# A routed attention and expert kernel: the third expert's token rows are requested ahead of two weight tiles, and their transposes and copies are written ahead of the weights' steps

## The chip, the cores and the metric

The kernel runs on one core of one Trainium2 chip. Its time is device microseconds of one execution. Each engine of the core works through its own queue of instructions in order: TensorE (PE, with its weight loads listed as PEld), VectorE (DVE), ScalarE (ACT), GpSimd (POOL) and SyncE (SP), which here only issues DMAs. An engine whose next instruction waits holds up all that is queued behind it.

## The reference

Three stages follow one another. An attention over 16 clusters gives 1536 token rows of 512 numbers. A mixture of experts sends each token to one of 8 experts, with two matrix products of 512x1024 and 1024x512. A gated convolution block ends it.

```python
for s in range(S):                       # for each of 2 batches, 768 tokens
    fresh_e = int(np.argmax(logits[b, s]))
    e = fresh_e if s == 0 or local_gate[b, s] < 0.5 else prev_e
    prev_e = e
    p = softmax(logits[b, s])
    h = np.maximum(x[b, s] @ w1[e], 0.0)
    out[b, s] = p[e] * (h @ w2[e])
...
gate = 1 / (1 + np.exp(-causal_conv5(x)))
return gate * (x @ w_val) @ w_out
```

The weights of an expert are 4 tiles of 128x2048 f32: two of w1 and two of w2.

## The kernel before

**Rows by expert.** At the end of attention the token rows (512 numbers, the probability and the token's number, 514 in all) are scattered into `xslots` in DRAM, one region for each expert. `load_x(k)` reads the rows of the expert at place k into a tile `xs`; even and odd places share one buffer each (`xs0`, `xs1`), so the rows of place 2 go into the buffer of place 0. Places 2 to 5 take their expert from a count made on the chip, which SP reads with `value_load`. `do_x(k)` copies the ids and probabilities on DVE, transposes the rows on PE into a single PSUM bank `xp`, and splits the result: `xhi` is the cast by ACT (L1135), `xlo` the remainder by DVE (L1137). Place 2 has 300 rows in pieces of 128, 108 and 64; it does this in two parts, and part 1 needs the bank that part 0 leaves.

**The products.** `do_mm1(k)` runs over two halves q of w1 and two pairs fp of column blocks in each; `do_mm2(k)` follows with w2. The order is mm1(0), mm2(0), mm1(1), mm1(2), mm2(1), mm1(3), mm2(2) and so on. Place 1's first product uses whole f32 tiles (`wone`); place 2's uses tiles that were split into `whi` (ACT, L360) and `wlo` (DVE, L366), and has three terms: xhi by whi, xlo by whi, xhi by wlo.

**The weights' steps.** `w_stage` requests a raw tile `wraw` on SP's queue; when it is in, `w_split` converts it in two halves. These conversions stand in a list `work`; `tick()`, called once for each pair fp and at places of mm2, takes one from it, then two small DVE steps of an overflow table (`late`), then one step of the conversion of the last block's weights (`wspace`: L260 is its load, L230 to L238 its DVE steps). The raw tiles of place 2's w1 are requested at L1251 and at L1275 (`w_stage(stg[0])`); `keep_rows(3)` (L1253) stores a plain copy of the last 384 rows to `xall`. In `do_mm1(0)` the request `load_x(2)` comes after all of these; in `do_mm1(1)` the two parts of `do_x(2)` come after the tick of their pair.

Of the kernel before, what the change touches and what calls it, by code (L numbers as in the profile page):

```python
# [21 lines left out]
E = 8  # L22
# [19 lines left out]
def routed_attention_moe_kernel(  # L42
# [267 lines left out]
    stg = [wstg]  # L310
# [10 lines left out]
    def w_load(j, t):  # L321
        k, i = worder[j]
        if k in AT:
            nc.sync.dma_start(t, wq[4 * AT[k] + i])
        else:
            nc.sync.dma_start(t, wq[bass.ds(turn[k] * 4 + i, 1)].rearrange("o p f -> (o p) f"))
# [5 lines left out]
    def w_stage(at):  # L332
        if pending:
            j = pending.pop(0)
            home[j] = at
            wraw[j] = at.tile([128, 2048], F32, tag="w", name="wraw")
            w_load(j, wraw[j])
# [175 lines left out]
    def keep_rows(gq):  # L513
        nc.sync.dma_start(
            xall[384 * gq:384 * gq + 384, :].rearrange("(t p) c -> p t c", p=128), xnat[:, 3 * gq:3 * gq + 3, :]
        )
# [530 lines left out]
    def tick():  # L1047
        for _ in range(pops[0]):
            if work:
                work.pop(0)()  # L1050
        for _ in range(2 if late else 0):
            if late:
                late.pop(0)()
        if conv and XS.get("ready"):
            conv.pop(0)()
            beats[0] += not late
            if conv and beats[0] % 2:
                conv.pop(0)()
# [15 lines left out]
    def halves(k):  # L1074
        cols = AT[k], E + HALVED.index(AT[k])
        return cols[::-1] if ROWS[AT[k]][0] == PACK else cols

    def load_x(k):
        if k >= E:
            return  # L1080
        n, rows = NT[k], TR[k]
        XS[k] = xs_p.tile([128, -(-WX[k % 2] // 128), XC], F32, tag=f"xs{k % 2}", name="xs")
        if k == 0:
            c = E + HALVED.index(AT[0])
            nc.sync.dma_start(XS[k][:CAPS[0], 0, :], xslots[c * SLOT:c * SLOT + CAPS[0], :])
            return
        if AT.get(k) in HALVED:
            for t, c in enumerate(halves(k)):
                nc.sync.dma_start(XS[k][:TR[k][t], t, :], xslots[c * SLOT:c * SLOT + TR[k][t], :])
            return  # L1090
        if k in AT:
            src = xslots[AT[k] * SLOT:AT[k] * SLOT + CAPS[k], :]
        else:
            src = xslots[bass.ds(turn[k] * SLOT, CAPS[k]), :]
        if FOLD[k] or k == 0:
            for t, r in enumerate(rows):
                nc.sync.dma_start(XS[k][:r, t, :], src[sum(rows[:t]):sum(rows[:t]) + r, :])
        else:
            nc.sync.dma_start(XS[k][:rows[0], :n, :], src.rearrange("(t p) c -> p t c", p=rows[0]))

    def do_x(k, part=0):
        n, w = NT[k], CAPS[k]
        same = [(slice(t, t + 1), r) for t, r in enumerate(TR[k])] if len(set(TR[k])) > 1 else [(slice(0, n), TR[k][0])]
        parts = 2 if w > 256 else 1
        if part >= parts:
            return
        xs = XS[k]
        if part == 0:
            ids = small.tile([128, 3], I32, tag="ids", name="ids", bufs=6)
            for ts, r in same:  # L1110
                nc.vector.tensor_copy(ids[:r, ts], xs[:r, ts, 513])
            pw = small.tile([128, 3], F32, tag="pw", name="pw", bufs=6)
            for ts, r in same:
                nc.vector.tensor_copy(pw[:r, ts], xs[:r, ts, 512])
            IDS[k], PW[k] = ids, pw
            XT[k] = [
                xt_p.tile([128, 4, WX[k % 2]], F32 if k in WHOLE else F32R, tag=f"x{s}{k % 2}", name=f"x{s}")
                for s in ("hi", "lo")[:1 if k in WHOLE else 2]
            ]
        hi = XT[k][0]  # L1120
        xp = ps_x.tile([128, 1024], F32, tag="x", name="xp").rearrange("p (d c) -> p d c", d=4 // parts)
        d0 = 2 * part
        for t, r in enumerate(TR[k]):
            c0 = sum(TR[k][:t])
            for d in range(4 // parts):
                nc.tensor.transpose(  # L1126
                    xp[:, d, c0:c0 + r], xs[:r, t, 128 * (d0 + d):128 * (d0 + d) + 128], ident[:r, :r]
                )
        qs = [(slice(2 * q, 2 * q + 2), slice(d0 + 2 * q, d0 + 2 * q + 2)) for q in range(2 // parts)]
        if k in WHOLE:  # L1130
            (a, c), (a2, c2) = qs
            nc.scalar.copy(hi[:, c, :w], xp[:, a, :w])  # L1132
            nc.vector.tensor_copy(hi[:, c2, :w], xp[:, a2, :w])
        for a, c in qs if k not in WHOLE else ():
            nc.scalar.copy(hi[:, c, :w], xp[:, a, :w])  # L1135
        for a, c in qs if k not in WHOLE else ():
            nc.vector.tensor_tensor(XT[k][1][:, c, :w], xp[:, a, :w], hi[:, c, :w].bitcast(F32), op=ALU.subtract)  # L1137
        if part == parts - 1:
            XS.pop(k)

    def do_mm1(k):
        w = CAPS[k]
        xs = XT.pop(k)
        h = HT[k] = h_p.tile([128, 8, 2 * WX[k % 2]], F32R, tag=f"h{k % 2}", name="h")
        c0 = w - PACK if FOLD[k] else w
        for q in range(2):
            if k in WHOLE:
                terms = [(W[k, q].rearrange("p (d f) -> p d f", d=4), xs[0])]
            else:
                whv, wlv = [t.rearrange("p (d f) -> p d f", d=4) for t in W[k, q]]  # L1150
                terms = [(whv, xs[0]), (whv, xs[1]), (wlv, xs[0])]
            for fp in range(2):
                if w > 256:
                    hps = [ps_h.tile([128, 1, 512], F32, tag="h", name="hps") for _ in range(2)]
                else:
                    hps = [ps_h.tile([128, 2, 256], F32, tag="h", name="hps")]
                for fi in range(2):
                    f = 2 * fp + fi
                    fs = slice(128 * f, 128 * f + 128)
                    hp = hps[fi][:, 0, :w] if w > 256 else hps[0][:, fi, :w]  # L1160
                    for n, (a, c) in enumerate(terms):
                        for d in range(4):
                            nc.tensor.matmul(  # L1163
                                hp, a[:, d, fs], c[:, d, :w], start=(n + d == 0), stop=(n + d == len(terms) + 2)
                            )
                m = 2 // len(hps)
                for i, hp in enumerate(hps):
                    fs = slice(4 * q + 2 * fp + m * i, 4 * q + 2 * fp + m * i + m)
                    hhi = h[:, fs, c0:c0 + w]
                    nc.scalar.activation(hhi, hp[:, :, :w], AF.Relu)  # L1170
                    for c1, c2, at_ in ((0, c0, 0), (c0, w, c0 + w)):
                        if c1 < c2:
                            nc.vector.scalar_tensor_tensor(
                                h[:, fs, at_:at_ + c2 - c1], hp[:, :, c1:c2], 0.0, hhi[:, :, c1:c2].bitcast(F32),
                                op0=ALU.max, op1=ALU.subtract,
                            )
                pops[0] = 2 if (k, q) >= (E - 1, 0) else 1
                tick()
                if k < E - 1 and (q, fp) in ((0, 1), (1, 0)):
                    do_x(k + 1, q)  # L1180
                    if q == 0:
                        load_x(k + 2)
            if k:
                queue_w(wpos[k, q])

# [62 lines left out]
    w_whole(R + 1, ring1)  # L1248
    for n, k in enumerate(free):
        turn[k] = nc.sync.value_load(ordi[0:1, n:n + 1], min_val=NF, max_val=E - 1)  # L1250
    w_stage(stg[1])  # L1251
    low.append(stg[2].tile([128, 2048], F32R, tag="w", name="wlo"))
    keep_rows(3)  # L1253
    high = [ring1.tile([128, 2048], F32R, tag="lo", name="whi") for _ in range(2)]
    for q in range(2):
        for c in (slice(0, 1024), slice(1024, 2048)):
# [2 lines left out]
    for q in range(2):  # L1259
        wv = W[0, 2 + q].rearrange("p (f d) -> p f d", f=4)  # L1260
        for f in range(4):
            fa = 4 * q + f
            if fa == 7:
                do_x(0)
            nc.tensor.matmul(ey, ehh[:, fa, :], wv[:, f, :], start=(fa == 0), stop=(fa == 7))
    y = y_p.tile([128, 512], F32, tag="y", name="ysb")
    nc.scalar.activation(y, ey, AF.Copy, scale=EA["pw"])
    scatter(x2d, EA["ids"], y, 2 * S, "rows of different tokens")
# [6 lines left out]
    w_stage(stg[0])  # L1275
    late += overflow_steps()
    do_mm1(0)
    do_mm2(0)
    queue_split(R + 2)
# [322 lines left out]
```

## Time and profile before

| | |
|---|---|
| median of 3 runs | 529.61 us (528.85 to 531.57) |
| the profiled execution | 530.8 us, of which the profile's span is 528.7 us |
| PE busy | 509.7 us, 96% of the span |
| DVE busy | 361.6 us, 68% |
| ACT busy | 312.8 us, 59% |
| DMA | 108.38 MB, mean 205 GB/s |

Times in rows are us from the start of the span. In a timeline a row has its start, its length, engine, line, operation, out<-in, shapes, the count of instructions merged, and in brackets the idle time before it and what ended it. SPq rows are the issue of a DMA, not its transfer. In a row of windows "PE busy (x)" is busy us and instructions; PEclk is the granted share of TensorE's clock (1.00 is 2.4 GHz, 0.50 is 1.2 GHz), then come the busy share of the DMA engines and the GB/s moved. A matmul of f32 stands in the trace as two records, so 16 records are one pair fp of place 1.

### The profile page before, as it was taken

To read this page: it belongs to the slowest core of one execution; us is meant where nothing else is said; L and a number is where in the kernel's file an instruction comes from. 1 tells how busy PE (TensorE), PEld (TensorE's weight loads), DVE (VectorE), ACT (ScalarE), POOL (GpSimd) and SP (SyncE) were. 2 spreads that over 40 slices of the span, in tenths; PEclk is the share of its full clock that TensorE was granted. 3 is DMA by queue.
4 is the path that set the end of the run, shared out by engine and by line. 5 is a ranking of instruction groups with operands and counts; after the bars stand their busy time and mean duration, and the time that the engine had idled before them with its cause. 6 is when DMAs were issued, how large, how long until landed. Compare 5 with 4: busy or idle time off the path is not lost. (4 is left out here: it accounts for less than half of the span.)

```text
span 528.7 us, 8832 instructions
## 1 busy us (share of the span) xinstructions
PE 509.7 (96%) x3189; PEld 405.7 (77%) x3190; DVE 361.6 (68%) x704; ACT 312.8 (59%) x597; POOL 95.0 (18%) x106
## 2 busy tenths in 40 slices
PE   7898999999999999999989899999999999999996
PEld 3675767777676777776859788979898886899885
DVE  6684767665687787554726489996875791599960
ACT  3596867777777767766332356645435373485642
POOL 5111002020103022000220003424435252000000
PEclk7899999999999999999999799999999999999999
DMA  5877687888977883840459945886999846730023
GB/s 146 232 150 225 140 263 207 220 260 197 316 161 267 203 263 79 235 172 0 111 192 338 349 119 194 282 301 226 365 326 349 310 156 234 235 136 2 20 100 119
DMA packets 35352, 108.38 MB, mean 205 GB/s; under 512 B 4666, under 2 KB 5178, under 8 KB 30697
## 3 DMA queue, kind: packets, MB, share of 16 engines
q1 hardware_dynamic: 32217, 100.90, 62.2%
q0 software_dynamic: 2128, 6.31, 3.2%
q10 hardware_dynamic: 960, 0.58, 0.4%
q8 instruction: 26, 0.43, 0.3%
q14 instruction: 21, 0.17, 0.1%
HBM read 58.14 MB, written 29.58 MB: 166 GB/s over the span
## 5 line engine op out<-in xcount | busy, mean ns | idle before, releaser
L675 DVE TENSOR_REDUCE mx<-s 128x1 f32<-128x768 f32 x96 | 91.5, 954 | 59.8 <-PE s L668 53.6
L704 ACT COPY pt<-tp 128x384 f32<-128x384 f32 x148 | 65.5, 482 | 55.8 <-PE tp L699 55.7
L684 ACT ACTIVATE pexp<-s,mx 128x768 f32<-128x768 f32 x96 | 87.0, 906 | 6.6 <-DVE mx L675 5.1
L699 PE MATMUL tp<-ident,pexp 128*128 128x128 f32 x576 | 80.8, 276 | 0.3 <-DVE pt L702 0.2
L699 PEld LDWEIGHTS tp<-ident,pexp 128*128 128x128 f32 x576 | 67.8, 141 | 7.7 <-ACT pt L704 3.3
L711 PE MATMUL pv<-pt,vt 128*64 128x384 f32 x360 | 67.8, 498 | 0.0
L366 DVE TENSOR_TENSOR wlo<-wraw,whi 128x1024 fp32r<-128x1024 f32 x40 | 55.4, 1393 | 11.7 <-ACT whi L360 11.4
L664 PE MATMUL s<-st 128*128 128x384 f32 x188 | 57.6, 388 | 1.7 <-ACT pexp L684 1.7
L668 PE MATMUL s<-st 80*128 80x384 f32 x188 | 48.8, 341 | 1.4 <-DMA st<-ohr 1.4
L1163 PE MATMUL hps<-xhi,wone 128*128 128x176 f32 (+3 forms) x320 | 48.4, 312 | 0.0
L1163 PEld LDWEIGHTS hps<-xhi,wone 128*128 128x128 f32 x320 | 46.9, 197 | 1.2 <-ACT xhi L1132 0.2
L360 ACT CAST whi<-wraw 128x1024 fp32r<-128x1024 f32 x40 | 40.6, 1044 | 10.0 <-PE yp L1200 5.1
L664 PEld LDWEIGHTS s<-st 128*128 128x128 f32 x188 | 28.8, 192 | 18.0 <-issue 7.3
L711 PEld LDWEIGHTS pv<-pt,vt 128*64 128x64 f32 x360 | 21.9, 136 | 23.8 <-issue 23.8
L1170 ACT ACTIVATE h<-hps 128x352 fp32r<-128x352 f32 (+6 forms) x36 | 16.2, 450 | 38.6 <-PE hps L1163 38.5
L668 PEld LDWEIGHTS s<-st 80*128 80x128 f32 x188 | 34.5, 191 | 1.7 <-issue 1.7
L1198 PE MATMUL yp<-whi,h 128*112 128x512 f32 (+5 forms) x88 | 34.9, 397 | 0.9 <-ACT h L1170 0.9
L384 POOL TENSOR_TENSOR xx<-xkq,xx 128x768 fp32r<-128x768 f32 x8 | 14.6, 1820 | 116.4 <-ACT xx L378 95.9
L1199 PE MATMUL yp<-wlo,h 128*112 128x512 f32 (+5 forms) x88 | 34.7, 394 | 0.0
L1200 PE MATMUL yp<-whi,h 128*112 128x512 f32 (+5 forms) x88 | 34.6, 394 | 0.0
L1423 DVE SCALAR_TENSOR_TENSOR gt<-xf,convw_sb,gt 128x768 f32<-128x768 f32 x32 | 31.9, 1013 | 0.4
L1206 ACT ACTIVATE ysb<-yp,pw 64x512 f32<-64x512 f32 (+6 forms) x16 | 11.0, 685 | 33.8 <-PE yp L1196 17.0
(280 smaller groups left out, 911.2 us busy)
## 6 DMA issues: line engine op xcount, KB each, us to landing
wraw<-in_wq_dram SPq DMA_DIRECT2D x20, 1024.0 KB
st<-xx SPq DMA_DIRECT2D x48, 384.0 KB
wone<-in_wq_dram SPq DMA_DIRECT2D x12, 1024.0 KB
xslots<-padrow SPq DMA_DIRECT2D x15, 771.0 KB
xkq<-in_kq_dram SPq DMA_DIRECT2D x15, 384.0 KB
wspace<-in_wd_dram SPq DMA_DIRECT2D x8, 512.0 KB
xall<-xnat SPq DMA_DIRECT2D x4, 771.0 KB
vt<-in_v_dram SPq DMA_DIRECT2D x8, 384.0 KB
```

Source lines behind the costliest of these rows:

```text
L360: nc.scalar.copy(hi[:, c], wraw[j][:, c])
L366: nc.vector.tensor_tensor(lo[:, c], t[:, c], hi[:, c].bitcast(F32), op=ALU.subtract)
L664: nc.tensor.matmul(ps[:, n, :384], st[:, 1, q0:q0 + 128], st[:, 0, 384 * n:384 * n + 384], start=True, stop=False)
L668: nc.tensor.matmul(ps[:, n, :384], st[0:80, 2, q0:q0 + 128], st[0:80, 3, 384 * n:384 * n + 384], start=False, stop=True)
L675: nc.vector.tensor_reduce(mx, ps[:, :, :384], axis=AX.XY, op=ALU.max, negate=True)
L684: nc.scalar.activation(pt, ps[:, :, :384], AF.Exp, bias=mx[:, 0:1], accum_out=Zt[i // 6][:, t, h:h + 1])
L699: nc.tensor.transpose(tp[:, k, :], p[:, 128 * kt:128 * kt + 128], ident)
L704: nc.scalar.copy(dst, tp)
L711: nc.tensor.matmul(PVs[u][64 * h:64 * h + 64, :], Vt[g][:, kt, h, :], PT[u, h][:, kt, :], start=(kt == 0), stop=(kt == NQT - 1), skip_grou ...
L1163: nc.tensor.matmul(hp, a[:, d, fs], c[:, d, :w], start=(n + d == 0), stop=(n + d == len(terms) + 2))
L1198: nc.tensor.matmul(yp[:r], h[:, fa, hi], whv[:, f, :], start=(q == 0 and f == 0), stop=False)
L1199: nc.tensor.matmul(yp[:r], h[:, fa, hi], wlv[:, f, :], start=False, stop=False)
```

## The change

`load_x(2)` is called right after the first expert's transposes are written, ahead of the request of place 2's first raw tile, of the plain copy of rows and of the second raw tile. (`w_stage(stg[1])` and `keep_rows(3)` move with it behind the early products in the program's text; on SP's queue nothing lies between.) In `do_mm1(1)` alone the two parts of `do_x(2)` now come before the tick of their pair. Other places keep their order.

```diff
@@ do_mm1
                 pops[0] = 2 if (k, q) >= (E - 1, 0) else 1
+                rows = k < E - 1 and (q, fp) in ((0, 1), (1, 0))
+                if rows and k == 1:
+                    do_x(k + 1, q)
                 tick()
-                if k < E - 1 and (q, fp) in ((0, 1), (1, 0)):
+                if rows and k != 1:
                     do_x(k + 1, q)
-                    if q == 0:
-                        load_x(k + 2)
+                if rows and k and q == 0:
+                    load_x(k + 2)
@@ before the early products
-    w_stage(stg[1])
     low.append(stg[2].tile([128, 2048], F32R, tag="w", name="wlo"))
-    keep_rows(3)
@@ after them
+    load_x(2)
+    w_stage(stg[1])
+    keep_rows(3)
     y = y_p.tile([128, 512], F32, tag="y", name="ysb")
```

On SP's queue, from the last of the four value loads to the fourth expert's rows, there stood before:

```order
L326 ISA
L326 DMA wraw<-in_wq_dram 128x2048
L514 DMA xall<-xnat 128x3x514
L326 ISA
L326 DMA wraw<-in_wq_dram 128x2048
L1097 ISA
L1097 DMA xs<-xslots 128x514
L1097 ISA
L1097 DMA xs<-xslots 108x514
L1097 ISA
L1097 DMA xs<-xslots 64x514
L324 DMA wraw<-in_wq_dram 128x2048
```

In the same stretch there stands now (`xs` are the third expert's rows, `wraw` raw weight tiles, `xall` the plain copy):

```order
L1097 ISA
L1097 DMA xs<-xslots 128x514
L1097 ISA
L1097 DMA xs<-xslots 108x514
L1097 ISA
L1097 DMA xs<-xslots 64x514
L326 ISA
L326 DMA wraw<-in_wq_dram 128x2048
L514 DMA xall<-xnat 128x3x514
L326 ISA
L326 DMA wraw<-in_wq_dram 128x2048
L324 DMA wraw<-in_wq_dram 128x2048
```

The three pieces of rows have moved past two tiles and the copy; what follows is as it was.

On DVE, in place 1's second half of w1, part 1 of the remainder `xlo` of place 2 moves (- before, + now):

```order
+L1137 TENSOR_TENSOR xlo<-xp,xhi 128x600
 L366 TENSOR_TENSOR wlo<-wraw,whi 128x1024
 L989 TENSOR_SCALAR own<-ce 128x11
 L230 TENSOR_SCALAR wspace<-wspace 128x512
 L231 SCALAR_TENSOR_TENSOR wspace<-wspace 128x512
-L1137 TENSOR_TENSOR xlo<-xp,xhi 128x600
 L1173 SCALAR_TENSOR_TENSOR h<-hps,h 128x2x112
```

It stood behind a conversion of weights, two table steps and two steps on `wspace`; now it stands ahead of them.

On ACT, in the same pairs, the casts `xhi` of place 2 and `whi` of the weights change places:

```order
 L1170 ACTIVATE h<-hps 128x2x176
 L360 CAST whi<-wraw 128x1024
 L1170 ACTIVATE h<-hps 128x2x176
-L360 CAST whi<-wraw 128x1024
 L1135 CAST xhi<-xp 128x600
-L1170 ACTIVATE h<-hps 128x2x176
 L360 CAST whi<-wraw 128x1024
+L1170 ACTIVATE h<-hps 128x2x176
 L1135 CAST xhi<-xp 128x600
+L360 CAST whi<-wraw 128x1024
 L1170 ACTIVATE h<-hps 128x2x176
```

The first cast of weights stays where it was; the two after it now wait until the rows' cast of their pair is done.

## Rows read from the trace of the kernel before

**Rows 1.** The page: PE's share of the span, granted clock in 40 slices.

```profile
PE 509.7 (96%) x3189; PEld 405.7 (77%) x3190; DVE 361.6 (68%) x704; ACT 312.8 (59%) x597; POOL 95.0 (18%) x106
...
PEclk7899999999999999999999799999999999999999
```

**Rows 2.** PE's timeline, from place 1's first product to place 2's second half.

```profile
289.87 4.93 PE L1163 MATMUL hps<-xhi,wone 128*128 128x176 f32 x32
296.66 0.41 PE L1126 MATMUL xp<-ident,xs 128*128 128x128 f32 x2 [1.85 <-DMA xs<-xslots]
297.85 1.02 PE L1126 MATMUL xp<-ident,xs 108*128 108x108 f32 x4 [0.79 <-DMA xs<-xslots]
298.81 5.06 PE L1163 MATMUL hps<-xhi,wone 128*128 128x176 f32 x16
303.66 1.26 PE L1126 MATMUL xp<-ident,xs 128*128 128x128 f32 x6
304.85 2.65 PE L1163 MATMUL hps<-xhi,wone 128*128 128x176 f32 x16
307.22 0.84 PE L1163 MATMUL hps<-xhi,whi 128*128 128x300 f32 x4
...
309.40 0.55 PE L1163 MATMUL hps<-xlo,whi 128*128 128x300 f32 x2 [1.07 <-DVE xlo L1137]
309.79 0.71 PE L1163 MATMUL hps<-xhi,wlo 128*128 128x300 f32 x4
...
315.32 0.98 PE L1126 MATMUL xp<-ident,xs 120*128 120x120 f32 x8
```

**Rows 3.** Windows: busy us (instructions) by engine, PEclk, DMA share, GB/s.

```profile
276.00:294.80 18.80, 18.25 (x127) 16.34 (x126) 10.49 (x37) 5.17 (x11) 2.21 (x2) 1.00 1.00 328
...
298.80:303.60 4.80, 4.80 (x17) 4.79 (x17) 0.78 (x1) 0.66 (x1) 0.00 (x0) 0.50 1.01 415
...
307.00:309.00 2.00, 1.33 (x10) 1.09 (x8) 1.47 (x3) 1.40 (x2) 0.00 (x0) 1.00 0.11 34
309.00:311.00 2.00, 1.60 (x11) 1.60 (x12) 2.00 (x5) 0.42 (x1) 0.00 (x0) 1.00 0.00 0
312.00:323.00 11.00, 11.00 (x83) 10.96 (x82) 10.47 (x29) 7.21 (x14) 1.37 (x1) 1.00 0.57 209
```

**Rows 4.** The chain that ended last, 250 to 330 us: start, length, what.

```profile
282.52 15.29 DMA xs<-xslots
```

**Rows 5.** SP's timeline, the requests around the third and fourth expert's rows.

```profile
279.79 0.37 SPq L326 DMA_DIRECT2D wraw<-in_wq_dram  x1
...
281.97 1.68 SPq L1097 DMA_DIRECT2D xs<-xslots  x3
...
292.18 0.34 SPq L260 DMA_DIRECT2D wspace<-in_wd_dram  x1
...
298.54 0.38 SPq L1099 DMA_DIRECT2D xs<-xslots  x1
311.00 7.53 SPq L326 DMA_DIRECT2D wraw<-in_wq_dram  x2
```

**Rows 6.** Waits of SP, 255 to 330 us: total, times, longest.

```profile
SPq L260 <- DMA xall<-xnat: 1.5, 1, 1.5
```

**Rows 7.** Timelines of ACT (first two) and DVE.

```profile
292.88 1.04 ACT L360 CAST whi<-wraw 128x1024 fp32r<-128x1024 f32 x1
...
298.97 0.66 ACT L1135 CAST xhi<-xp 128x600 fp32r<-128x600 f32 x1 [2.73 <-PE xp L1126]
...
299.66 0.78 DVE L1137 TENSOR_TENSOR xlo<-xp,xhi 128x600 fp32r<-128x600 f32 x1 [1.09 <-ACT xhi L1135]
304.40 0.59 DVE L1173 SCALAR_TENSOR_TENSOR h<-hps,h 128x224 fp32r<-128x224 f32 x2 [3.96 <-ACT h L1170]
305.33 1.23 DVE L366 TENSOR_TENSOR wlo<-wraw,whi 128x1024 fp32r<-128x1024 f32 x1 [0.34 <-ACT whi L360]
...
308.57 0.77 DVE L1137 TENSOR_TENSOR xlo<-xp,xhi 128x600 fp32r<-128x600 f32 x1
```

## The prediction

> **What bounds the kernel now.** The page comes first: PE is busy for 96% of the span, and its granted clock has one slice at 7 late in the run, the 23rd, 291 to 304 us [rows 1]. So a change can gain only where PE stands, or where it is busy at a lower clock. PE's timeline shows both in that slice [rows 2]. Before the third expert's transposes PE waits 1.85 us and then 0.79 us for its rows `xs`. The pair fp that follows takes from 298.81 to 303.66, 4.85 us, while the same 16 records from 304.85 to 307.22 take 2.37 us. The windows say why: between 298.8 and 303.6 the granted clock is 0.50, the 1.2 GHz level [rows 3]; PE had just stood for most of 3 us. Last, inside place 2's first product PE waits 1.07 us for `xlo` of DVE. From 309.40 on I see no wait until the fourth expert's transposes at 315.32 [rows 2]. The chain names the source: 15.29 us from the issue of the second piece of rows to PE's transposes [rows 4].
>
> **Requests in the new order.** The three pieces are issued from 281.97, the first of the two tiles at 279.79 [rows 5]. From 276.0 to 294.8 the DMA engines are busy for a share of 1.00 and move 328 GB/s [rows 3], so a request lands when the bytes ahead of it are through. Two tiles of 128x2048x4 bytes (1.05 MB each) and the copy of 384x514x4 (0.79 MB) go from ahead of the rows to behind them: 2.89 MB, at 328 GB/s 8.8 us. The first piece then lets PE start at 296.66 - 8.8 = 287.9, the second at 297.85 - 8.8 = 289.1. PE asks at 294.6 (below): about 5 us to spare, and the waits of 1.85 and 0.79 go. The other end: if requests shared the engines instead of queueing, the rows would gain only their earlier issue, 281.97 - 279.79 = 2.2 us, and PE could start the first at 294.5 and the second at 295.7, a wait of about 1 us. I take the first end, since the share of 1.00 is a queue that never empties; the second stays in the range.
>
> What is late next is what was passed. 300 rows of 514x4 bytes are 0.62 MB, 1.9 us at the same rate; the bound above is that plus 1.7 us of issue [rows 5], 3.6 us. SP's request of 292.18 was the one that waited for the copy `xall` [rows 5, 6], so the copy had landed by 292.1, and the first tile, 0.79 MB ahead of it, by 289.7; with 1.9 us more, 291.6. Its first cast ran at 292.88 without a wait [rows 7]: 1.3 us of cover. The second tile follows the copy by 1.05 MB, 295.3, and now 297.2; its cast comes at about 299.5. I cost both at nothing; by the upper bound the first cast would be 0.4 us late, still ahead of the rows' cast that follows it on ACT. SP itself stands for `xall` until about 294 in place of 292.1, with a tile's request behind it that is not due before 298.5.
>
> **Rows ahead of weights.** In the second pair of that half, `xlo` of part 1 starts on DVE at 308.57, behind the remainder of weights of 305.33, two table steps and two steps on `wspace` [rows 7]. Moved ahead, it follows its own cast: PE's transposes end near 298.5, the cast takes 0.66 and `xlo` 0.78 [rows 7], so it is ready by about 300.4, and PE needs it at 301.3. The 1.07 us go. In the first pair, casts and remainders of the weights' second half stand behind the rows' instead: `wlo` ends near 298.7, where PE needs it after 301. The tightest place is the bank `xp`: part 1's transposes, due at 297.7, need part 0's `xlo`, done near 297.4.
>
> **PE's path.** From the start at 289.87 [rows 2]: two pairs of 2.37 us, 294.6; six transposes, 0.7 us (eight of 120 rows took 0.98 with their drain), 295.3; a pair, 297.7; six transposes, 298.4; a pair, 300.75. Then place 2's first half: from 309.79 to 315.32 ran 10 of its 12 groups of four, 0.553 us each, so 12 take 6.64 us, and PE comes to the fourth expert's transposes at 307.4, where it came at 315.32. That is 7.9 us: 2.64 of waits, 1.07 of the later wait, the rest the clock.
>
> **The new wait.** Those rows are the last request, at 298.54, before SP's next at 311.00 [rows 5]. The DMA share falls to 0.11 between 307 and 309 and is 0.00 from 309 to 311 [rows 3]: they land close to 309. The new order leaves the bytes ahead of them as they were, on a queue that is full until they are through; their own request, which follows DVE's second half of `wlo`, comes perhaps 1.2 us later, under that cover. So PE waits from 307.4 until 309.1, 1.7 us, and 7.9 - 1.7 = 6.2 us are left.
>
> The Trainium skill ("DMA: Bandwidth & Descriptors", section "Queues, rings and completion order") has every DMA engine take descriptors in the order of its ring, while completions need not keep it. By its first half the rows of the third expert gain all 8.8 us and those of the fourth nothing, which speaks against the full 7.9 us; if instead small requests went beside large ones, the third's would gain 2.2 us and the fourth's could come sooner.
>
> **What follows.** After 309 the same instructions run. DVE is nearly as loaded as PE there (10.47 of 11.00 us [rows 3]), so it must come earlier by as much. It can: it stood 1.09 us before part 0's `xlo` and 3.96 us before the next evacuation [rows 7], and both go, so that the evacuation of 304.40 comes near 299.0. DVE gains at least 5.4 us, and a lag of 0 to 0.8 us behind PE's 6.2 could reach PE; I take 0, because PE's new wait gives DVE time.
>
> **Sum.** The profiled execution took 530.8 us, span 528.7 and 2.1 around it. 530.8 - 6.2 = 524.6. Against the median of 529.61 it would be 523.4; the half-clock stretch need not be as long in each run, and where it was shorter less is gained, so I take 524.2.
>
> **Rivals.**
> 1. The clock falls again, now at the new wait. For: 2.64 us of waits within 3.1 us did it. Against: 1.07 us did not, the clock is 1.00 behind it [rows 3]; 1.7 us lies between. The price from the two pairs: 2.48 us for a pair at half clock, with the transposes up to 3.4, or half of it for a stretch half as long, 1.7. Gain 2.8 to 4.5, time 525.9 to 527.6.
> 2. No new wait: the fourth's rows come before 307.4, or PE is there later by small waits and loses nothing. At most 7.9 us gained, 522.5.
> 3. The weights take the rows' place: a tile lands over 2 us later than I have it, or requests share the engines, and PE stands before place 2's product with its clock falling as now. 2.5 us of wait and 3.4 of clock come back from the 6.2: 529.5 to 530.
> 4. Slower: the fourth's rows come late. SP serves in order, and their request now stands behind the copy's landing and DVE's `wlo`, both later than now. Every us beyond 309 is a us of wait; from 315.3 on, 6.3 us later than now, the kernel is slower (from 312 on if the clock also falls, 3.4 us). With 9 us it is 533.
> 5. The change does nothing: the rows' buffer is that of the first expert, and the request could wait for it. Its transposes were over before 279.8, so it does not; counted with 3.
>
> **How the numbers follow.** Forecast 0.50, by itself 522.8 to 525.6; rival 1 0.22; rival 2 0.10; rivals 3 and 5 0.13; rival 4 0.05. What a measurement tells from no change is 0.5%, 2.65 us. Faster: 0.50, 0.10, nearly all of rival 1 and a little of 3, 0.83. The rest of rivals 1 and 3 is no change, 0.12; slower 0.05. The range goes from below rival 2 to past the end of rival 1: 522.0 to 528.0.
>
> **What would show it.** Right: no wait for `xs` before the third expert's transposes, full clock from 294 to 307, `xlo` no longer a releaser of PE, mm1 of place 2 beginning near 301, a wait of 1 to 2 us for `xs` before the fourth's transposes near 307.5, which begin near 309. Wrong: a wait for `whi` or `wlo` near 301, a clock of 0.50 after 309 (rival 1), or the fourth's rows landing well away from 309.

## The result, and the profile after

The changed kernel took 524.37 us in the median of 5 runs (522.96 to 524.75), the kernel before 529.61 us beside it (528.18 to 531.57). The ratio is 0.989, 95% interval 0.9861 to 0.9918: 5.2 us less, between 4.3 and 7.4. The profiled execution took 524.34 us with a span of 522.3 us, against 530.8 and 528.7.

The page of the changed kernel: PE's share of the span, and the granted clock in 40 slices.

```profile
PE 507.6 (97%) x3189; PEld 403.6 (77%) x3190; DVE 360.1 (69%) x704; ACT 313.3 (60%) x597; POOL 96.7 (19%) x106
...
PEclk9899999999999999999999999999999999999999
```

The slice at 7 late in the run [rows 1] is gone. The low slices at the start are in both kernels.

PE's timeline over the stretch of [rows 2]:

```profile
291.00 4.94 PE L1163 MATMUL hps<-xhi,wone 128*128 128x176 f32 x32
295.77 0.83 PE L1126 MATMUL xp<-ident,xs 128*128 128x128 f32 x6
296.54 2.65 PE L1163 MATMUL hps<-xhi,wone 128*128 128x176 f32 x16
299.03 0.83 PE L1126 MATMUL xp<-ident,xs 128*128 128x128 f32 x6
299.79 2.65 PE L1163 MATMUL hps<-xhi,wone 128*128 128x176 f32 x16
302.16 0.84 PE L1163 MATMUL hps<-xhi,whi 128*128 128x300 f32 x4
302.85 0.71 PE L1163 MATMUL hps<-xlo,whi 128*128 128x300 f32 x4
...
308.93 0.98 PE L1126 MATMUL xp<-ident,xs 120*128 120x120 f32 x8
...
315.86 0.72 PE L1163 MATMUL hps<-xhi,wlo 128*128 128x300 f32 x4
```

No row has a bracket: PE waits for nothing between 291.00 and the fourth expert's transposes. That stretch takes 308.93 - 291.00 = 17.93 us, where it took 315.32 - 289.87 = 25.45 us [rows 2]: 7.52 us less. From those transposes to the end of the span both kernels take the same, 528.7 - 315.32 = 213.4 and 522.3 - 308.93 = 213.4 us. Against the 7.52 us stands that place 1's first product starts 1.13 us later here, at 291.00. Nothing that was changed comes before it on PE. The difference is there by attention's first score product (L664, at 19.12 us against 18.03) and varies from run to run: in the later profiles of the same kernel and its variants place 1's product starts between 289.1 and 290.8. 7.52 - 1.13 = 6.4, the difference of the spans. It is more than the 5.2 us of the medians, since the profiled execution of the kernel before lies 1.2 us above its median (530.8 against 529.61) and that of the changed kernel at its own.

Windows of the changed kernel, columns as in [rows 3]:

```profile
295.00:307.00 12.00, 12.00 (x86) 11.58 (x85) 10.67 (x29) 7.20 (x12) 0.00 (x0) 1.00 0.88 332
300.00:301.00 1.00, 1.00 (x8) 1.00 (x8) 0.74 (x3) 1.00 (x2) 0.00 (x0) 1.00 0.48 111
307.00:309.00 2.00, 2.00 (x17) 2.00 (x16) 2.00 (x7) 0.60 (x2) 0.00 (x0) 1.00 0.78 197
```

PE is busy for all 14 us from 295 to 309 at a granted clock of 1.00, the 2.4 GHz level; in [rows 3] the pair behind the wait ran at 0.50. The DMA engines have a gap here at 300 to 301, a share of 0.48, where before they were busy throughout (1.01 from 298.8 to 303.6 [rows 3]). The requests on SP's queue, against [rows 5]:

```profile
281.07 2.08 SPq L1097 DMA_DIRECT2D xs<-xslots  x3
283.35 0.42 SPq L326 DMA_DIRECT2D wraw<-in_wq_dram  x1
...
296.01 0.34 SPq L260 DMA_DIRECT2D wspace<-in_wd_dram  x1
299.59 0.33 SPq L324 DMA_DIRECT2D wraw<-in_wq_dram  x1
...
300.61 0.38 SPq L1099 DMA_DIRECT2D xs<-xslots  x1
306.51 7.04 SPq L326 DMA_DIRECT2D wraw<-in_wq_dram  x2
```

Of the last request of rows (L1099, the fourth expert's) the list of DMA issues says how long it took to land: KB, then us.

```profile
xs<-xslots SPq DMA_DIRECT2D x1, 481.9 KB, 7.8
```

So these rows were in at 300.61 + 7.8 = 308.4, half a microsecond before PE asked for them at 308.93.

The request of L260, which waits for the plain copy, came 5.0 us after the start of place 1's product, where it came 2.3 us after it before: the copy is later by 2.7 us, and PE waits for nothing that is behind it. On ACT (first two rows, casts of the first and the second tile) and DVE:

```profile
294.01 1.04 ACT L360 CAST whi<-wraw 128x1024 fp32r<-128x1024 f32 x1
...
300.46 1.05 ACT L360 CAST whi<-wraw 128x1024 fp32r<-128x1024 f32 x1
...
297.39 0.78 DVE L1137 TENSOR_TENSOR xlo<-xp,xhi 128x600 fp32r<-128x600 f32 x1
298.34 1.23 DVE L366 TENSOR_TENSOR wlo<-wraw,whi 128x1024 fp32r<-128x1024 f32 x1 [0.16 <-ACT whi L360]
...
300.59 0.78 DVE L1137 TENSOR_TENSOR xlo<-xp,xhi 128x600 fp32r<-128x600 f32 x1 [0.26 <-ACT xhi L1135]
301.54 1.23 DVE L366 TENSOR_TENSOR wlo<-wraw,whi 128x1024 fp32r<-128x1024 f32 x1 [0.16 <-ACT whi L360]
```

Neither cast has a bracket: both tiles were in when their casts came up. Part 1's `xlo` is done at 301.4, 1.5 us before PE's first matmul on it (302.85). DVE's idle times of 1.09 and 3.96 us [rows 7] are gone; between these rows it stands 0.26 us at most.

### The profile page after: what moved, and what is told of

The parts are those of the page before. It is cut to its first block, busy times and chain, and to the rows that moved or that the text cites. A ratio compares the mean times of both kernels' runs of the same rounds, so it can differ in the third digit from the quotient of the medians.

```text
span 522.3 us, 8829 instructions
## 1 busy us (share of the span) xinstructions
PE 507.6 (97%) x3189; PEld 403.6 (77%) x3190; DVE 360.1 (69%) x704; ACT 313.3 (60%) x597; POOL 96.7 (19%) x106
## 5 line engine op out<-in xcount | busy, mean ns | idle before, releaser
L664 PE MATMUL s<-st 128*128 128x384 f32 x188 | 57.3, 386 | 1.5 <-ACT pexp L684 1.5
L1163 PE MATMUL hps<-xhi,wone 128*128 128x176 f32 (+3 forms) x320 | 46.0, 302 | 0.0
L1163 PEld LDWEIGHTS hps<-xhi,wone 128*128 128x128 f32 x320 | 44.7, 190 | 1.1 <-ACT xhi L1132 0.2
L664 PEld LDWEIGHTS s<-st 128*128 128x128 f32 x188 | 28.6, 191 | 17.8 <-issue 7.3
```

Source lines behind the costliest of these rows:

```text
L664: nc.tensor.matmul(ps[:, n, :384], st[:, 1, q0:q0 + 128], st[:, 0, 384 * n:384 * n + 384], start=True, stop=False)
L1163: nc.tensor.matmul(hp, a[:, d, fs], c[:, d, :w], start=(n + d == 0), stop=(n + d == len(terms) + 2))
```

## The experiments

Each kernel was timed with the kernel before on the same chip; its median there was 529.87, 530.28 and 529.62 us in the three groups of runs. "Path" is the time from the start of place 1's first product to the fourth expert's transposes on PE, 25.45 us before and 17.93 after.

**The requests alone.** The steps go back to their old order.

```diff
-                if rows and k == 1:
-                    do_x(k + 1, q)
                 tick()
-                if rows and k != 1:
+                if rows:
                     do_x(k + 1, q)
```

> The new order of requests with the old order of steps. Theory A (the gain is PE's time before place 2's products: waits for rows, the half clock behind them, the wait for xlo): rows early, full clock, but xlo of part 1 stands on DVE behind a weight remainder and two steps on wspace again, while PE comes about 5 us sooner. By the changed kernel's trace xlo would be ready near 305.0 where PE needs it at 302.85: a wait of about 2 us for xlo, so 2 us slower than the changed kernel, 526.4 us. Rival B (the order of requests alone makes the gain, the order of steps adds nothing): 524.4 us, no wait for xlo over 0.3 us.

525.31 us (524.35 to 526.35), ratio 0.992 (0.9891 to 0.9948). PE's timeline (first two rows) and DVE's:

```profile
298.38 0.89 PE L1126 MATMUL xp<-ident,xs 128*128 128x128 f32 x6 [0.81 <-DVE xlo L1137]
...
303.10 0.54 PE L1163 MATMUL hps<-xlo,whi 128*128 128x300 f32 x2 [0.41 <-DVE xlo L1137]
...
297.56 0.77 DVE L1137 TENSOR_TENSOR xlo<-xp,xhi 128x600 fp32r<-128x600 f32 x1
...
302.27 0.78 DVE L1137 TENSOR_TENSOR xlo<-xp,xhi 128x600 fp32r<-128x600 f32 x1
```

The path is 309.01 - 289.37 = 19.64 us, 1.7 more than with both parts. On the trace rival B falls: the order of steps does add something, once the rows are early. My 2 us for the wait on part 1's `xlo` was too much, 0.41; the larger wait, 0.81, is for the single bank `xp`, which part 0's `xlo` releases. The prediction called that bank the tightest place, but I had not named it in the expectation. In time the difference is 0.9 us, the intervals of the two ratios overlap, so the profile and not the clock on the wall carries this point.

**The steps alone.** The old requests, with the new order in `do_mm1(1)`.

```diff
+                rows = k < E - 1 and (q, fp) in ((0, 1), (1, 0))
+                if rows and k == 1:
+                    do_x(k + 1, q)
                 tick()
-                if k < E - 1 and (q, fp) in ((0, 1), (1, 0)):
+                if rows and k != 1:
                     do_x(k + 1, q)
-                    if q == 0:
-                        load_x(k + 2)
+                if rows and q == 0:
+                    load_x(k + 2)
```

> The old order of requests with the new order of steps. Theory A: PE still waits 2.6 us for rows and its clock falls to 0.50 for about 7 us; only the 1.07 us wait for xlo goes: 528.5 us, 1.1 below the kernel before. Rival C (the order of steps makes most of the gain): 525 to 526 us. Against both: DVE's copies of ids stand for the rows with a weight remainder behind them, which would show as a wait of PE for wlo and a time above 529.6 us.

527.05 us (525.47 to 530.05), ratio 0.995 (0.9924 to 0.9976). PE's timeline, a row of windows, and one row of SP's timeline here followed by the same request in the kernel before:

```profile
297.20 0.41 PE L1126 MATMUL xp<-ident,xs 128*128 128x128 f32 x2 [2.77 <-DMA xs<-xslots]
298.31 0.92 PE L1126 MATMUL xp<-ident,xs 108*128 108x108 f32 x4 [0.70 <-DMA xs<-xslots]
299.16 4.09 PE L1163 MATMUL hps<-xhi,wone 128*128 128x176 f32 x16
```
```profile
298.80:302.00 3.20, 3.20 (x12) 3.08 (x13) 2.08 (x6) 1.61 (x2) 0.00 (x0) 0.50 0.23 93
```
```profile
302.21 0.33 SPq L324 DMA_DIRECT2D wraw<-in_wq_dram  x1
...
297.52 0.33 SPq L324 DMA_DIRECT2D wraw<-in_wq_dram  x1
```

The wait for rows and the half clock stay and the wait for `xlo` goes, as A said, but the half clock lasts 3.4 us (298.7 to 302.1), not 7. The path is 312.99 - 289.49 = 23.50 us, 1.95 less than before, though the wait for rows is 0.8 us longer: here the half-clock stretch is over before the second group of transposes, where it covered them before. So of 2.8 us in time not all is the order of steps. The time lies between A's 528.5 and rival C's 525 to 526; C, the steps as most of the gain, falls by the paths: the requests alone bring it to 19.64 us, the steps to 23.50. In the medians they gain 4.6 and 2.8 us, with intervals that overlap; together that is more than both parts gain, so in part they gain the same. The rows' copies hold DVE's remainder of weights, and with it the next requests: SP issues at 302.21 what it issued at 297.52 before, and the DMA share falls to 0.23. That cost PE nothing, since it was late itself.

**The wait filled.** The kernel before, with work for PE while it waits.

```diff
                 if k < E - 1 and (q, fp) in ((0, 1), (1, 0)):
+                    if (k, q) == (1, 0):
+                        keep_warm(ps_y.tile([128, 512], F32, tag="y", name="spin2"), 8)
                     do_x(k + 1, q)
```

> The kernel before, with 8 extra matmuls of 128x512 (result unused) ahead of the third expert's transposes of part 0, which fill about 1.7 us of the 2.6 us for which PE waits for rows. Theory A (the half clock is the larger part of what the wait costs): the wait as such stays, rows still let PE start near 296.7 and 297.9, but the clock stays at 1.00 behind it: 2.5 us for the pair and about 0.6 us for the transposes come back, 526.5 us. Rival D (the slow pair has another cause, such as the DMA traffic of those microseconds): the pair still takes 4.85 us, 529.6 us.

528.13 us (527.19 to 530.02), ratio 0.9976 (0.9958 to 0.9993). PE's timeline and a row of windows:

```profile
294.67 1.89 PE L117 MATMUL spin<-onesb 128*128 128x512 bf16 x8
...
297.85 2.65 PE L1163 MATMUL hps<-xhi,wone 128*128 128x176 f32 x16
300.34 0.83 PE L1126 MATMUL xp<-ident,xs 128*128 128x128 f32 x6
...
306.03 0.55 PE L1163 MATMUL hps<-xlo,whi 128*128 128x300 f32 x2 [1.44 <-DVE xlo L1137]
```
```profile
297.00:300.00 3.00, 2.79 (x18) 2.56 (x19) 1.94 (x10) 0.66 (x1) 0.00 (x0) 1.00 1.01 388
```

Rival D falls: with the DMA engines as busy as before (1.01), the pair goes at full clock, 300.34 - 297.85 = 2.49 us. The path is 311.95 - 289.90 = 22.05 us, 3.40 less than the profiled kernel before, close to the 3.1 us expected. In the medians it is 1.7 us, 0.4 to 2.2 by the interval. The profiled execution of the kernel before lies 0.9 us above this group's median, that of the filled wait (527.32) 0.8 us below its own, which makes up the difference. The clock is one reason. In the profiled kernel before it was at 0.50 for 6.8 us here (297.7 to 304.6). The granted clock of every run, as a mean over its span, is on record: 0.9891 in the mean of the 20 runs before, 0.9925 in the 12 with the filled wait. The difference, 0.0034 of 529 us, is 1.8 us of clock lost, or 3.6 us at half clock (standard error 1.7): the mean stretch was about half as long as the profiled one.

**The rows in third place**, behind one tile and the copy.

```diff
-    load_x(2)
     w_stage(stg[1])
     keep_rows(3)
+    load_x(2)
```

> The changed kernel with the third expert's rows behind the first tile and the copy, ahead of the second tile alone. Theory A (a request lands when the bytes ahead of it are through): rows gain 1.05 MB at 328 GB/s, 3.2 us, against the kernel before; PE can start the first piece at 293.5 and the second at 294.7 where it asks at 294.6, no wait over 0.3 us, full clock, 524.4 us as the changed kernel. Rival E (requests share the engines, what counts is the moment of issue): the rows gain only some 0.5 us of issue, PE waits about 2 us for them, the clock falls, 528 us or more.

523.80 us (522.90 to 525.31), ratio 0.9887 (0.9858 to 0.9917). PE's timeline:

```profile
290.81 4.94 PE L1163 MATMUL hps<-xhi,wone 128*128 128x176 f32 x32
295.58 0.93 PE L1126 MATMUL xp<-ident,xs 128*128 128x128 f32 x6
296.44 2.65 PE L1163 MATMUL hps<-xhi,wone 128*128 128x176 f32 x16
```

and its weight loads (PEld):

```profile
296.17 0.20 PEld L1126 LDWEIGHTS xp<-ident,xs 64*128 64x128 f32 x2 [0.23 <-DMA xs<-xslots]
```

No wait but 0.23 us for the last piece, so the rows came just in time; full clock, the time of the changed kernel. The request is issued at 282.13, 8.7 us ahead of place 1's product, where it was 7.9 us ahead (281.97 [rows 5]): 0.8 us sooner, while PE waited 2.6 us for the rows before. So rival E, by which the moment of issue counts, falls. Passing one tile of 1.05 MB is enough; passing the first tile and the copy as well bought nothing more. The Trainium skill ("DMA: Bandwidth & Descriptors", "Queues, rings and completion order") has each DMA engine take descriptors in the order of its ring; these rows agree with it.

**The fourth expert's rows sooner.**

```diff
                 if rows and k == 1:
                     do_x(k + 1, q)
+                if rows and k == 1 and q == 0:
+                    load_x(k + 2)
                 tick()
...
-                if rows and k and q == 0:
+                if rows and k > 1 and q == 0:
                     load_x(k + 2)
```

> The changed kernel with the fourth expert's rows requested one step sooner, ahead of a weight tile and a part of the last block's weights (1.57 MB, 4.8 us at 328 GB/s). Theory F (as its trace shows, the fourth's rows land 0.5 us before PE asks, so no wait is left to remove): 524.4 us, within 0.5 us of the changed kernel, rows in by about 304. Rival G (in most executions PE does wait 1 to 2 us there, as the prediction had it, and the profiled one was lucky): 522.7 to 523.4 us.

523.92 us (522.43 to 524.53), ratio 0.9887 (0.9856 to 0.9918); path 307.04 - 289.11 = 17.93 us. F holds and G falls: the time is that of the changed kernel, no wait was there to remove.

**The fourth expert's rows later**, behind the next weight tile.

```diff
-                if rows and k and q == 0:
+                if rows and k > 1 and q == 0 or k == 1 and (q, fp) == (1, 1):
                     load_x(k + 2)
```

> The changed kernel with the fourth expert's rows requested two ticks later, behind the next weight tile, whose own request waits for DVE's second remainder of the tile before (306.5 in the changed kernel's trace). Both theories of the prediction's rivals are priced by it. Theory H (wait and clock add): the rows land near 312.5, PE waits 3.5 us at 308.9 and its clock falls behind that wait, 1.7 to 3.4 us more: 529.6 to 531.3 us, all of the gain given back. Rival I (a wait costs only its own length, the clock stays): 528 us. Rival J (rows of 0.5 MB are through soon after their issue, whatever stands ahead): wait under 1 us, 525.3 us.

530.30 us (528.86 to 531.57), ratio 1.0011 (0.9989 to 1.0032). PE's timeline and two rows of windows:

```profile
312.09 1.86 PE L1126 MATMUL xp<-ident,xs 120*128 120x120 f32 x8 [4.61 <-DMA xs<-xslots]
313.61 1.35 PE L1163 MATMUL hps<-xhi,whi 128*128 128x300 f32 x4
314.76 1.20 PE L1163 MATMUL hps<-xlo,whi 128*128 128x300 f32 x4
315.76 1.20 PE L1163 MATMUL hps<-xhi,wlo 128*128 128x300 f32 x4
...
321.72 0.72 PE L1163 MATMUL hps<-xhi,wlo 128*128 128x300 f32 x4
```
```profile
311.20:314.00 2.80, 1.91 (x9) 1.91 (x10) 1.23 (x6) 0.01 (x1) 0.00 (x0) 0.50 0.39 126
...
318.00:323.00 5.00, 5.00 (x36) 4.83 (x36) 2.95 (x6) 3.24 (x7) 1.87 (x2) 1.00 0.00 0
```

H holds, with a wait of 4.61 us in place of 3.5: the granted clock falls to 0.50, groups of four take 1.00 us (314.76 to 315.76) where they take 0.55, and the whole gain is gone. From the transposes to the last group of place 2's first product it takes 321.72 - 312.09 = 9.63 us, in the changed kernel 315.86 - 308.93 = 6.93: the half clock costs 2.7 us here, beside the wait. So rival I, by which the clock stays, falls, and with it J, by which there is hardly a wait. This is the prediction's rival 4 at the place it named, short of slower.

**Rows ahead of weights at all places.**

```diff
-                if rows and k == 1:
+                if rows and k:
                     do_x(k + 1, q)
                 tick()
-                if rows and k != 1:
+                if rows and not k:
                     do_x(k + 1, q)
```

> The changed kernel with rows ahead of weights at all places from 1 on, not at place 1 alone. Theory K (the order of steps pays only where PE comes to xlo before DVE does, and after place 1 PE shows no such wait): 524.4 us, within 0.5 us of the changed kernel. Rival L (the weights' steps, later by an evacuation of about 2 us on DVE at each place, become what PE waits for): a wait for wlo of 0.5 to 1 us a place, 526 to 528 us.

523.12 us (522.28 to 523.94), ratio 0.9875 (0.9844 to 0.9905), path 307.63 - 289.70 = 17.93 us. No wait for `wlo` appeared, so L falls. The 1.2 us below the changed kernel's median looked like more than K allows, so both were run again on one chip, this one together with the sooner request:

> The changed kernel with both of the last variants: rows ahead of weights at all places, the fourth expert's request one step sooner. Theory M (nothing that PE waits for is left to move here, differences of about 1 us between these kernels come from the run): within 0.5 us of the changed kernel timed beside it, both 523 to 524.5 us. Rival N (the 523.1 us with rows ahead at all places was a gain of its own): 1 us or more below the changed kernel, 522.5 us or less.

> The changed kernel once more, on the same chip as the variant with rows first. Theory M: 523 to 524.5 us, PE at the fourth expert's transposes 17.9 us after place 1's first product starts, no wait there or one under 0.5 us. Rival G (a wait of 1 to 2 us for the fourth's rows in most executions): its profile shows that wait, 524.5 us or more.

Both variants together took 523.62 us (522.77 to 524.61), ratio 0.9887 (0.9857 to 0.9917); the changed kernel beside it 523.54 us (522.27 to 526.31), ratio 0.9886 (0.9851 to 0.9921). M holds: they are the same, and no version was found that beats the changed kernel. Its second profile, on PE:

```profile
308.07 0.98 PE L1126 MATMUL xp<-ident,xs 120*128 120x120 f32 x8
```

Again no wait, 308.07 - 290.14 = 17.93 us after the start of place 1's product.

## Why the prediction was right, and where it was not

**The time and its main cause were right.** 524.37 us was measured, 524.2 predicted. The waits of 1.85, 0.79 and 1.07 us went; so did the half clock. The filled wait shows that the clock is a cost of its own, the third place that the bytes ahead of a request count for its landing and not its moment of issue, and the run with requests alone, by its trace, that the steps' order is needed once the rows are early.

**The step that failed is the new wait of 1.7 us for the fourth expert's rows.** I let them land at 309, 19.1 us after the start of place 1's product, and PE ask after 17.5. PE asked after 17.93 us, 0.4 later than my sum: a pair takes 2.49 us where transposes follow it, not 2.37, each six transposes 0.77, not 0.7, and place 2's first half 6.77, not 6.64. The rows were in after 308.4 - 291.00 = 17.4 us, 1.7 us sooner than I let them be. The premise that failed is the queue that stays full until they are through: it had room at 300 to 301 (0.48). None of the four profiles with both parts and this request in its place (the changed kernel twice, third place, all places) has a wait there. So rival 2, to which I gave 0.10, is what the trace shows, with a path 7.5 us shorter, not 6.2.

**Why the number came out all the same.** Two sizes offset the missing wait. In the profiled pair the changed kernel began place 1's product 1.13 us later by the run. In the medians the half clock is worth less than in the profiled kernel before: 1.7 us against 3.4 by the filled wait. For that I had allowed 0.8 us (524.2 in place of 523.4). 7.5 less 1.7 is 5.8 us; 5.2 was measured, and 6.1 in the last group of runs, so the agreement within 0.2 us is luck.

**The cover held.** The first tile, for whose cast I saw 1.3 us to spare, was in when it came up; the second tile and the late copy made PE wait for nothing; DVE kept up with PE. Rivals 1, 3, 4 and 5 did not come. The clock did not fall after 309 because there was no wait, so the changed kernel says nothing on whether 1.7 us would have done it.

**What stays open** is why the rows passed sooner. They did not begin sooner: by the packets of the trace, 2056 bytes for each row, the first of the fourth's rows started 13.6 us after place 1's first product before and 13.9 after; the last ended 18.7 us after it before and 16.6 after. So they passed in 5.1 us before, and in 4.9 with the filled wait, but in 2.7 to 3.4 us in the changed kernel (both profiles), with the requests alone, in third place, with rows ahead at all places and with the steps alone. In these six profiles the DMA share had fallen under 0.8 in some microsecond from 8 to 12 us after the product's start; in the two slow ones it was 0.92 or more in all of them. A queue that had room and rows that pass fast go together, but no run tests whether one makes the other. The mean packet of rows and copies of rows over the whole stretch (1,164 of them) took 124 ns before, 117 with the filled wait, 103 after, 106 with the requests alone; in third place it was 121 ns, and the rows were in time all the same, so shorter packets are not the whole of it.

## What to carry to other kernels

On a full DMA queue look for the small request that is needed first and stands behind large ones that are needed later; what it passes comes later (the copy by 2.7 us here, with 1.9 us of bytes put ahead of it), and passing just enough is enough. Count a wait of the matmul engine with the clock that it may take down, but take that price from several runs. When a wait goes, follow the engine to the next thing it asks for: here that came with half a microsecond to spare, and requesting it two steps later gave back the whole gain.

## What the runs showed of the hardware

The granted clock fell to 0.50 behind waits of 1.85 and 0.79 us with one group of transposes between them (before), 2.77 and 0.70 (steps alone) and 4.61 us (fourth's rows later). It stayed at 1.00 behind 1.07 us (before), 0.81 and 0.41 (requests alone) and 0.43 and 1.44 us (filled wait). The half-clock stretch lasted 6.8 us before (297.7 to 304.6), 3.4 us with the steps alone (298.7 to 302.1), though its waits were longer, and 6.8 us with the fourth's rows later (311.1 to 318.0). So in these three the price does not follow the length of the wait.
